# Top-32 attention into an MLP on one core: wider weight pieces, diagonals on another engine, other places for scores and values, and turns by DMA

## The chip, the core and the metric

The kernel runs on one core of one Trainium2 chip. The time is the device time of one execution in microseconds (us); the times before are given as the median of three runs. A core has these engines: PE (TensorE, matrix products; its weight loads are shown as PEld), DVE (VectorE), ACT (ScalarE), POOL (GpSimd) and SP (SyncE, which here only issues DMAs). Each works through its own queue of instructions in order, and waits where an instruction needs something that another engine or a DMA has not delivered yet.

## The reference

Inputs are q, k and v of 8 batches, 8 heads, 576 positions, 64 wide, and two weight matrices, `w_in` (512 x 2048) and `w_out` (2048 x 512). The weights come as 64-bit floats, all else as 32-bit floats.

```python
scores = scale * np.matmul(q, k.transpose(0, 1, 3, 2))
kth = np.partition(scores, -32, axis=-1)[..., -32:-31]
scores = np.where(scores >= kth, scores, -1e9)
attn = softmax(scores)                        # over the keys
x = np.matmul(attn, v)                        # (B,H,S,D) -> (B*S, H*D) = 4608 x 512
h = x @ w_in
g = np.where(h >= 1, h, np.where(h <= -1, 0.0, (h + 1) ** 2 / 4))
out = g @ w_out
```

Each query keeps its 32 largest scores of 576; the result of attention goes through a two-layer MLP.

## The kernel before

**Steps.** Attention is cut into 144 steps. A step is 128 queries of a pair of heads: its scores against 576 keys are two tiles of 128 x 576. Four steps (four head pairs) complete one chunk of 128 tokens by 512; there are 36 chunks. Batches go in pairs: four rounds of four steps for the first, two rounds of two steps for the last 64 queries of both (the tail rounds), four rounds of four steps for the second. A round's queries are turned (brought to columns) once.

**What a step does.** PE multiplies queries and keys into `sp` (L351), ACT scales that into `s` (L352). DVE takes the larger and the smaller of each column pair (`more` and `less`, L365, each reading two halves of `s`), and finds the largest scores eight at a time (MAX8 and MATCH_REPLACE8, L413 to L432), the 32nd by a scan (L444). ACT takes the exponential `e` (L388) with the negated maximum (`nmax`, L386). DVE masks `e` and sums it (L451), and inverts the sum (L397). What follows depends on the step. In the first nine ("early") steps and the last ones, ACT writes a diagonal matrix of the inverse sums (`diag`, L401), and PE multiplies the weights by it, which turns and divides them in one (`pw` L466, `pwt` L472); ACT copies the result to `wT` (L469, L473). In all others POOL divides (L404), ACT splits the words into 16-bit halves (`halves`, L481), and SP writes them to DRAM (`rows`, L483) and reads them back turned (`wT`, L484). Then PE multiplies values and weights (`po`, L498 and L506), and ACT copies that to a chunk's `xT` (L511).

**The MLP.** A chunk is 128 units of PE work. `hidden(x)` makes two products' worth of hidden values in a bank `ph` (L531), from which ACT makes `r` and `g` (L535, L542) and POOL the activation (L547 to L549); `final(f)` adds one product to `py` (L554), four hidden groups behind. `ph` and `po` share three banks. Units wait in a deque, `pending`.

**Weights.** They are converted from 64-bit words in pieces of 128 x 256 (64 pieces): ACT makes `units` (L145, L146), DVE `bits` (L154), POOL adds the two (L156). There are three buffers for each. `convert` issues the next piece's ACT part and the present piece's DVE and POOL part. Four pieces are done ahead of the first step; then each early step converts seven. While that lasts, the loads use eight rooms in the buffers `kT` and `v_in` (hence those names at L154 in the profile). Later each piece is loaded again and inspected (L171).

**The order of the work.** The order on PE, DVE, ACT and POOL is written out by hand: the program's order is each engine's order. A planner loop goes through the steps, each in seven slots. Per slot it issues one part of the step's selection on DVE, a conversion (early), and at fixed slots the transpose (slot 1), the values (slot 2) and the scores of step m + 2 (slot 4 in an early step, slot 2 otherwise); the queries and the next batch's keys are prepared at slot 6 or slot 1. At the end of each slot `advance` issues pending MLP units, as far as a share has come due and modelled times allow. In an early step the share is 48 units. SP's order (all DMAs) is not by hand: a scheduler sets it.

**Keys and queries.** For the first two batches PE turns the keys (`pk` L250, `pkt` L258, copied by ACT at L254 and L263) and the queries (`pq` L325, copied at L327). For later batches ACT splits them into halves (`parts`, L276, one buffer), SP writes `lines` (L278) and reads them turned (L279). The values' loads are issued among the turns of the keys.

Of the kernel before, what the change touches and what calls it, by code (L numbers as in the profile page):

```python
# [26 lines left out]
def kernel(  # L27
# [78 lines left out]
    WC = 256  # L106
    n_pieces = NK * DFF // WC + NF * DM // WC
    n_steps = B * (NT * NHP + NHP // 2)
    excess = const.tile([P, 2 * n_steps + n_pieces], F32, name="excess")
    signs = const.tile([P, 2, n_pieces], F32, name="signs")  # L110
# [15 lines left out]
    def load(pool, i, bufs=3):  # L126
        if i < n_pieces and i not in loaded:
            if room:
                loaded[i] = room[i % 8]
            else:  # L130
                loaded[i] = pool.tile([P, 2 * WC], U32, name="raw", bufs=bufs)
            nc.sync.dma_start(out=loaded[i], in_=pieces_of_weights[i][1].bitcast(U32))

    def words_of(pool, i, bufs=3):
        load(pool, i, bufs)
        words = loaded.pop(i).rearrange("p (n t) -> p n t", t=2)
        return words[:, :, 0], words[:, :, 1]

    def convert_piece(pool, i, any_size):

        lo, hi = words_of(pool, i)
        dst = pieces_of_weights[i][0]
        units = pool.tile([P, WC], F32, name="units", bufs=3)
        if not any_size:
            nc.scalar.activation(units, lo, AF.Identity, bias=one, scale=2.0 ** -52)  # L145
            nc.scalar.activation(units.bitcast(BF16).rearrange("p (n t) -> p n t", t=2)[:, :, 1], hi.bitcast(F32), AF.Sign)  # L146
        else:
            nc.scalar.activation(units, lo, AF.Identity, bias=two, scale=2.0 ** -51)
            sign = pool.tile([P, WC], F32, name="sign", bufs=3)
            nc.scalar.activation(sign, hi.bitcast(F32), AF.Sign)  # L150
        yield

        bits = pool.tile([P, WC], U32, name="bits", bufs=3)
        nc.vector.tensor_scalar(bits, hi, 3, None, ALU.logical_shift_left)  # L154
        if not any_size:
            nc.gpsimd.tensor_tensor(out=dst.bitcast(I32), in0=bits.bitcast(I32), in1=units.bitcast(I32), op=ALU.add)  # L156
        else:
            nc.gpsimd.tensor_tensor(out=bits.bitcast(I32), in0=bits.bitcast(I32), in1=units.bitcast(I32), op=ALU.add)
            size = pool.tile([P, WC], F32, name="units", bufs=3)
            nc.scalar.activation(size, hi.bitcast(F32), AF.Abs)  # L160
            nc.vector.scalar_tensor_tensor(out=sign, in0=size, scalar=TINY, in1=sign, op0=ALU.is_ge, op1=ALU.mult)

            nc.vector.tensor_scalar(bits.bitcast(F32), bits.bitcast(F32), LARGEST, -LARGEST, ALU.min, ALU.max)
            nc.gpsimd.tensor_tensor(out=dst, in0=sign, in1=bits.bitcast(F32), op=ALU.mult)
        yield

    def inspect_piece(pool, i):

        lo, hi = words_of(pool, i, 1)
        for x in range(2):  # L170
            nc.scalar.activation(lo.bitcast(F32), hi.bitcast(F32), AF.Sign, bias=tiny[:, x:x + 1],  # L171
                                 accum_out=signs[:, x, i:i + 1])


    def run(ctx, paired):
# [12 lines left out]
        def load_values(b):  # L188
# [6 lines left out]
            for j in range(2):  # L195
                nc.sync.dma_start(out=v_tl[0][j * TL:(j + 1) * TL, j::2, :],
                                  in_=v[b, j::2, SM:S, :].rearrange("h p d -> p h d"))
            for hp in range(NHP):
                g = hp % 2
                nc.sync.dma_start(out=v_tl[1][g * TL:(g + 1) * TL, 2 * hp:2 * hp + 2, :],  # L200
                                  in_=v[b, 2 * hp:2 * hp + 2, SM:S, :].rearrange("h p d -> p h d"))
            yield
# [69 lines left out]
        def turn(x, dst):  # L272
# [6 lines left out]
            nc.sync.dma_start_transpose(dst.bitcast(U16), lines.rearrange("p t k -> (p t) k"))  # L279

        def turned_keys_of(b):
# [15 lines left out]
            blocks = {0: load_block(0)}  # L297
            yield got
            for c in range(NT + 1):
                if c < NT:  # L300
                    blocks[c + 1] = load_block(c + 1)
                n = P if c < NT else TL
                turn(blocks.pop(c)[0:n], kT[:, :, c * P:c * P + n])
                if c == 1:
                    loads = load_values(b)
                    got["v"], got["v_tl"] = next(loads)
                if 1 <= c < NT:
                    next(loads)
                elif c == NT:
                    for _ in loads:  # L310
                        pass
                yield got
# [82 lines left out]
        def divide(st):  # L395
            rz = att.tile([P, 2], F32, name="rz")
            nc.vector.reciprocal(rz, st["z"])  # L397
            if st["by_tensor"]:
                st["rz"] = diag = (late or words).tile([P, 2, P], F32, name="diag", tag="halves", bufs=1)
                for i in range(2):  # L400
                    nc.scalar.activation(diag[:, i, :], ident, AF.Copy, scale=rz[:, i:i + 1])  # L401
# [75 lines left out]
        def move_w(st):  # L477
# [5 lines left out]
            nc.sync.dma_start(out=rows, in_=halves)  # L483
            nc.sync.dma_start_transpose(wT.bitcast(U16), rows.rearrange("p t k -> (p t) k"))  # L484
# [117 lines left out]
        def convert(time):  # L602
# [9 lines left out]
            for i in range(begun, converted + (7 if room else 3)):  # L612
                load(words, i)

        def inspect():
            nonlocal inspected
            if paired and inspected < n_pieces:
# [4 lines left out]
        K_TIME, PIECE_TIME, UNIT_TIME, SLOTS, EARLY_SHARE = 10.1, 0.55, 0.218, 7, 48  # L622
        pe_time, dve_time, done, scored, ready_at, usable = 9.0, 12.0, {}, {}, {}, {0: 0.0}

        def advance(amount, until):

            nonlocal spent, due, pe_time
            due = due + amount if pending else 0.0
            pe_time = max(pe_time, until - 4.0)
            while pending:  # L630
                cost, pieces, work, _ = pending[0]
                if pieces > converted or usable[pieces] > pe_time + 0.5:
                    break
                if due < cost or pe_time >= until:
                    break
                pending.popleft()
                due -= cost
                spent += cost
                pe_time += cost * UNIT_TIME
                work()  # L640
# [13 lines left out]
        if paired:  # L654
            for x in (stage.tile([P, NHP, S], F32, name="kT").rearrange("p h n -> p (h n)"),
                      stage.tile([P, H, NT, D], F32, name="v_in").rearrange("p h c d -> p (h c d)")):
                room.extend(x[:, c:c + 2 * WC].bitcast(U32) for c in range(0, 8 * WC, 2 * WC))
# [8 lines left out]
        prep = None  # L666
        state = []

        def queries(m):
            nonlocal pe_time  # L670
            if m < n and steps[m][0:2] not in qTs:
                r = steps[m][0:2]
                if r[0] > 1:
# [24 lines left out]
        for i in range(2, 8 if room else 3):  # L698
# [5 lines left out]
        for i in range(3):  # L704
            convert(13.0)
# [21 lines left out]
        for m in range(n + 2):  # L727
# [14 lines left out]
            if m < n:  # L742
# [3 lines left out]
                now_converting = range(SLOTS)  # L746
# [3 lines left out]
            for slot in range(SLOTS):  # L750
# [6 lines left out]
                elif slot == 3 and late is not None:  # L757
                    if m % 2:
                        inspect()
                    elif paired:  # L760
                        load(late, inspected, 1)
# [4 lines left out]
                if slot == 3 and 1 <= m <= n and state[m - 1] is not None and not state[m - 1]["by_tensor"]:  # L766
                    move_w(state[m - 1])
                    ready_at[m - 1] = done[m - 1] + 15.0
                if slot == 2 and m == n and paired:
# [5 lines left out]
                if slot == 2 and not early:  # L775
                    values_until((m - 2) // 2 * 2)
                if slot == (4 if early else 2):
                    begin_at(m + 2)
                if slot == (6 if early else 1):
                    queries(m + 3)  # L780
                    if (m < n and prep is None and next_keys < B and steps[m][0] == next_keys - 1 and steps[m][1] >= 1
                            and (next_keys > 1 or converted == n_pieces)):
                        prep = (turned_keys_of if next_keys > 1 else keys_of)(next_keys)
                    if prep is not None and (m % 2 == 0 or next_keys == 1):
                        got = next(prep, None)
                        pe_time += 0.5 if next_keys < 2 else 0.0
                        if got is None:
                            prep, next_keys = None, next_keys + 1
                        else:
                            keys[next_keys] = got  # L790
                advance((EARLY_SHARE if early else share) / SLOTS if m < n else 32.0, now)
# [52 lines left out]
```

## Time and profile before

| what | value |
|---|---|
| median of three runs | 1515.24 us |
| lowest and highest | 1515.05 and 1516.16 us |
| the profiled execution, its own time | 1516.81 us |
| the profile's span of it | 1514.6 us |
| mean granted clock of TensorE | 0.98 |
| moved by DMA | 259.76 MB, 172 GB/s |
| scans of DVE (L444), first, second and last | 24.83, 36.47 and 1440.08 us |
| end of PE's work | 1507.9 us |

The profile is of one execution. Its page gives the busy time of each engine, the span in 40 slices, the chain of work that ended last, and the costliest groups of instructions; further views answer by stretch of time, by wait (who waited, for whom, in total, how often, the longest), and by engine in order of time. A wait's releaser is inferred: it is the one that came last.

### The profile page before, as it was taken

What the parts mean: (1) busy time and instruction counts of PE and PEld (TensorE: products, weight loads), DVE (VectorE), ACT (ScalarE), POOL (GpSimd) and SP (SyncE); (2) the same over time, 40 slices, a digit from 0 to 9 for tenths busy, and PEclk for the clock granted to TensorE, in tenths of its full rate; (3) what the DMA queues carried; (4) which work ended last, traced back from release to release, by engine and by line L of the source; (5) the groups of instructions that cost most, each with busy time, mean ns of one, the idle gap of its engine ahead of it and who ended that gap; (6) DMA issues with size and microseconds to landing.
All of it is one profiled execution on the core that took longest, in us unless ns stands there. A gap on an engine that the chain in (4) does not pass through costs nothing.

```text
span 1514.6 us, 32180 instructions
## 1 busy us (share of the span) xinstructions
PE 1441.9 (95%) x10625; PEld 1042.8 (69%) x10625; DVE 1412.7 (93%) x4424; ACT 1167.1 (77%) x2288; POOL 921.8 (61%) x1339
## 2 busy tenths in 40 slices
PE   5588999999999999999999999899999999999998
PEld 4466677777777777677777777666677777777675
DVE  7888999999999999999999999999999999999912
ACT  7896878787778888787778888677777887777732
POOL 4563666666666666566666666566666666666630
PEclk7798999999999999999999999999999999999999
DMA  9542567775687777886677877786677777656510
GB/s 258 159 136 61 147 173 177 194 199 160 166 190 202 197 195 187 206 205 171 167 199 199 201 185 189 183 215 172 162 198 179 208 181 179 160 157 153 143 29 17
DMA packets 512448, 259.76 MB, mean 172 GB/s; under 512 B 459152, under 2 KB 467344, under 8 KB 512272
## 3 DMA queue, kind: packets, MB, share of 16 engines
q1 hardware_dynamic: 512272, 257.62, 65.6%
q8 instruction: 86, 1.41, 0.4%
q14 instruction: 90, 0.74, 0.2%
HBM read 62.91 MB, written 102.04 MB: 109 GB/s over the span
## 4 chain that ended last, share of the span: by engine, by line
PE 85%; ACT 8%; DMA 2%; issue 2%; POOL 1%; DVE 0%; SPq 0%; ACTq 0%; POOLq 0%; DVEq 0%
PE py L554 32%; PE ph L531 30%; PE sp L351 10%; PE po L498 10%; PE pw L466 2%; ACT halves L481 1%; ACT e L388 1%; ACT units L145 1%; PE po L506 1%; DMA rows<-halves 1%; ACT s L352 1%; DMA wT<-rows 1%; ACT wT L469 1%; ACT raw L171 0%; ACT g L542 0%
## 5 line engine op out<-in xcount | busy, mean ns | idle before, releaser
L531 PEld LDWEIGHTS ph<-xT,w_in 128*128 128x128 f32 x4608 | 547.0, 192 | 101.7 <-issue 82.2
L531 PE MATMUL ph<-xT,w_in 128*128 128x128 f32 x4608 | 557.2, 276 | 3.2 <-POOL w_in L156 3.1
L554 PE MATMUL py<-w_out,g 128*128 128x512 f32 x1152 | 551.0, 603 | 0.0
L547 POOL TENSOR_SCALAR r<-r 128x256 f32<-128x256 f32 x276 | 161.5, 585 | 447.2 <-ACT r L535 447.1
L372 DVE MATCH_REPLACE8 more<-tops,more 128x288 f32<-128x288 f32 x864 | 375.1, 437 | 0.0
L554 PEld LDWEIGHTS py<-w_out,g 128*128 128x128 f32 x1152 | 198.1, 191 | 181.2 <-issue 165.3
L481 ACT COPY halves<-e 128x1152 uint16<-128x1152 uint16 x266 | 291.9, 1143 | 15.5 <-DMA rows<-halves 14.5
L451 DVE SCALAR_TENSOR_TENSOR e<-s,kth,e 128x577 f32<-128x577 f32 x288 | 251.8, 909 | 3.6 <-ACT e L388 3.5
L549 POOL TENSOR_TENSOR g<-r,g 128x256 f32<-128x256 f32 x280 | 227.8, 814 | 22.0
L535 ACT ACTIVATE r<-ph,half 128x256 f32<-128x256 f32 (+1 forms) x296 | 136.1, 460 | 130.3 <-PE ph L531 104.2
L388 ACT ACTIVATE e<-s,nmax 128x576 f32<-128x576 f32 x288 | 222.4, 773 | 4.7
L404 POOL TENSOR_SCALAR e<-e,rz 128x576 f32<-128x576 f32 x266 | 223.4, 850 | 0.0
L352 ACT ACTIVATE s<-sp 128x576 f32<-128x576 f32 x288 | 172.0, 650 | 52.4 <-PE sp L351 51.9
L548 POOL TENSOR_TENSOR r<-r 128x256 f32<-128x256 f32 x276 | 191.3, 693 | 23.0
L351 PE MATMUL sp<-kT,qT 64*128 64x288 f32 x1024 | 162.9, 434 | 10.9 <-ACT kT L254 9.5
L498 PE MATMUL po<-wT,v_in 128*64 128x128 f32 x2048 | 143.4, 281 | 17.3 <-ACT g L542 15.3
L498 PEld LDWEIGHTS po<-wT,v_in 128*64 128x64 f32 x2048 | 117.0, 140 | 52.4 <-ACT g L542 40.1
L351 PEld LDWEIGHTS sp<-kT,qT 64*128 64x128 f32 x1024 | 89.4, 188 | 66.6 <-ACT r L535 25.0
L542 ACT ACTIVATE g<-ph,minus 128x256 f32<-128x256 f32 x280 | 130.1, 465 | 0.0
L413 DVE MAX8 tops<-more 128x8 f32<-128x288 f32 x288 | 125.4, 443 | 0.0
L365 DVE TENSOR_TENSOR less<-s 128x576 f32<-128x576 f32 x144 | 123.8, 860 | 0.0
L365 DVE TENSOR_TENSOR more<-s 128x576 f32<-128x576 f32 x144 | 109.9, 763 | 11.9 <-ACT s L352 11.9
(88 smaller groups left out, 1397.7 us busy)
## 6 DMA issues: line engine op xcount, KB each, us to landing
rows<-halves SPq DMA_DIRECT2D x133, 576.0 KB, 3.0
lines<-parts SPq DMA_DIRECT2D x48, 256.0 KB, 2.8
q_in<-in_q_dram SPq DMA_DIRECT2D x32, 256.0 KB, 4.0
kT<-in_moe_w_in_dram SPq DMA_DIRECT2D x32, 256.0 KB, 3.2
v_in<-in_moe_w_out_dram SPq DMA_DIRECT2D x32, 256.0 KB, 3.2
v_in<-in_v_dram SPq DMA_DIRECT2D x32, 256.0 KB, 4.2
raw<-in_moe_w_in_dram SPq DMA_DIRECT2D x32, 256.0 KB, 3.1
out_dram<-y SPq DMA_DIRECT2D x32, 256.0 KB, 3.2
```

The source lines that it names most:

```text
L351: nc.tensor.matmul(*x, start=True, stop=True)
L365: nc.vector.tensor_tensor(out=x, in0=s[:, :, 0:SH], in1=s[:, :, SH:S], op=op)
L372: nc.vector.match_replace(out=st["rest"][:, i, :], in_to_replace=eight(st["tops"], i, r - 8), in_values=src[:, i, :], imm_value=LOWEST)
L388: nc.scalar.activation(e[:, i, :], s[:, i, :], AF.Exp, bias=nmax[:, i:i + 1])
L404: nc.gpsimd.tensor_scalar(st["e"][:, i, :], st["e"][:, i, :], rz[:, i:i + 1], 1.0, ALU.mult, ALU.mult)
L451: nc.vector.scalar_tensor_tensor(out=st["all"][1][:, i, :], in0=st["all"][0][:, i, :], scalar=last[i], in1=st["all"][1][:, i, :], op0=ALU. ...
L481: nc.scalar.copy(halves[:, :, i * S:(i + 1) * S], st["e"][:, i, :].bitcast(U16).rearrange("p (k t) -> p t k", t=2))
L498: nc.tensor.matmul(po[j * D:(j + 1) * D], v_in[:, h, c, :] if c < NT else v_tl[0][:, h, :], wT[:, block(j, c)], start=(c == 0), stop=(c == ...
L531: nc.tensor.matmul(ph[:, i], w_in[:, kk, f * P:(f + 1) * P], xT[:, kk], start=(kk == 0), stop=(kk == NK - 1))
L548: nc.gpsimd.tensor_tensor(out=r, in0=r, in1=r, op=ALU.mult)
L549: nc.gpsimd.tensor_tensor(out=g, in0=r, in1=g, op=ALU.add)
L554: nc.tensor.matmul(py[0], gs[f // group][:, f % group], w_out[:, f, :], start=(f == 0), stop=(f == NF - 1))
```

## The change

1. Pieces of the weights are 512 wide: 32 pieces, two ahead of the first step, four in an early step (slots 0, 2, 4, 6), so eight early steps; four rooms for loads. The inspection keeps 256 (`parts=2`), and the modelled time of a piece becomes 0.9.
2. `diag` is written by GpSimd in place of ACT.
3. The scores of step m + 2 go out at slot 2 in every step, right behind the values.
4. Ahead of the values of a later step, at even m, pending units are issued until one final has gone out, if the last one was a hidden.
5. The turned read of `lines` is put off: it goes out at slot 3, or between a step's `rows` and its `wT`. The values' loads leave the keys' turns and go out in the steps that have none.
6. The second batch's keys are turned by DMA like those of later batches, and their preparation begins with the last early step; the queries are turned by DMA from the second late step on.

One more thing follows from 5: the six loads of the second batch's last 64 values are not issued in the changed program, because the third batch's loads take their place in `value_loads` first.

```diff
-    WC = 256
+    WC = 512
...
-    excess = const.tile([P, 2 * n_steps + n_pieces], F32, name="excess")
-    signs = const.tile([P, 2, n_pieces], F32, name="signs")
+    excess = const.tile([P, 2 * n_steps + 2 * n_pieces], F32, name="excess")
+    signs = const.tile([P, 2, 2 * n_pieces], F32, name="signs")
...
-    def load(pool, i, bufs=3):
-        if i < n_pieces and i not in loaded:
+    def load(pool, i, bufs=3, parts=1):
+        if i < n_pieces * parts and i not in loaded:
             if room:
-                loaded[i] = room[i % 8]
+                loaded[i] = room[i % len(room)]
             else:
-                loaded[i] = pool.tile([P, 2 * WC], U32, name="raw", bufs=bufs)
-            nc.sync.dma_start(out=loaded[i], in_=pieces_of_weights[i][1].bitcast(U32))
+                loaded[i] = pool.tile([P, 2 * WC // parts], U32, name="raw", bufs=min(bufs, 2))
+            c = i % parts * (WC // parts)
+            nc.sync.dma_start(out=loaded[i], in_=pieces_of_weights[i // parts][1][:, c:c + WC // parts].bitcast(U32))
...
-            nc.sync.dma_start_transpose(dst.bitcast(U16), lines.rearrange("p t k -> (p t) k"))
+            turns.append(partial(nc.sync.dma_start_transpose, dst.bitcast(U16), lines.rearrange("p t k -> (p t) k")))
+
+        turns = []
+
+        def finish_turns():
+            while turns:
+                turns.pop(0)()
...
             blocks = {0: load_block(0)}
+            got["loads"] = load_values(b)
+            got["v"], got["v_tl"] = next(got["loads"])
             yield got
...
-                if c == 1:
-                    loads = load_values(b)
-                    got["v"], got["v_tl"] = next(loads)
-                if 1 <= c < NT:
-                    next(loads)
-                elif c == NT:
-                    for _ in loads:
-                        pass
                 yield got
...
-                    nc.scalar.activation(diag[:, i, :], ident, AF.Copy, scale=rz[:, i:i + 1])
+                    nc.gpsimd.tensor_scalar(diag[:, i, :], ident, rz[:, i:i + 1], 1.0, ALU.mult, ALU.mult)
...
             nc.sync.dma_start(out=rows, in_=halves)
+            finish_turns()
             nc.sync.dma_start_transpose(wT.bitcast(U16), rows.rearrange("p t k -> (p t) k"))
...
-        K_TIME, PIECE_TIME, UNIT_TIME, SLOTS, EARLY_SHARE = 10.1, 0.55, 0.218, 7, 48
+        K_TIME, PIECE_TIME, UNIT_TIME, SLOTS, EARLY_SHARE = 10.1, 0.9, 0.218, 7, 48
...
+        def take():
+
+            nonlocal spent, due, pe_time, taken
+            cost, pieces, work, _ = pending[0]
+            if pieces > converted or usable[pieces] > pe_time + 0.5:
+                return False
+            pending.popleft()
+            due -= cost
+            spent += cost
+            pe_time += cost * UNIT_TIME
+            work()
+            taken = work.func
+            return True
...
-                if r[0] > 1:
+                if late is not None:
                     qTs[r] = turned_queries_of(q_ins[r], r[1])
...
-        for i in range(3):
-            convert(13.0)
+        convert(13.0)
...
-                now_converting = range(SLOTS)
+                now_converting = range(0, SLOTS, 2)
...
+                if slot == 3:
+                    finish_turns()
...
                 if slot == 2 and not early:
+                    if m % 2 == 0:
+                        while pending and taken is not None and taken.__name__ == "hidden" and take():
+                            pass
                     values_until((m - 2) // 2 * 2)
-                if slot == (4 if early else 2):
+                if slot == 2:
                     begin_at(m + 2)
                 if slot == (6 if early else 1):
                     queries(m + 3)
...
-                        prep = (turned_keys_of if next_keys > 1 else keys_of)(next_keys)
+                        prep = turned_keys_of(next_keys)
                     if prep is not None and (m % 2 == 0 or next_keys == 1):
                         got = next(prep, None)
-                        pe_time += 0.5 if next_keys < 2 else 0.0
                         if got is None:
                             prep, next_keys = None, next_keys + 1
                         else:
                             keys[next_keys] = got
+                            value_loads = got.get("loads", value_loads)
+                    elif value_loads is not None:
+                        next(value_loads, None)
```

## The prediction

> **What bounds the kernel now.** I read the page's shares first, then the table of stretches, the waits, and the timelines of single engines.
>
> ```profile
> PE 1441.9 (95%) x10625; PEld 1042.8 (69%) x10625; DVE 1412.7 (93%) x4424; ACT 1167.1 (77%) x2288; POOL 921.8 (61%) x1339
> ...
> PE 85%; ACT 8%; DMA 2%; issue 2%; POOL 1%; DVE 0%; SPq 0%; ACTq 0%; POOLq 0%; DVEq 0%
> ```
>
> PE and DVE are both nearly full, and the chain that ends last is PE's. The table of stretches (columns: stretch, then busy time of PE, PEld, DVE, ACT, POOL, then granted clock) shows two regimes:
>
> ```profile
> 20.00:40.00 20.00, 11.33 (x62) 7.45 (x60) 19.29 (x62) 17.77 (x39) 9.02 (x11) 0.59 0.84 249
> 40.00:60.00 20.00, 10.29 (x62) 8.51 (x63) 17.48 (x58) 17.62 (x42) 11.66 (x14) 0.75 0.57 174
> ...
> 120.00:140.00 20.00, 14.75 (x92) 11.30 (x89) 15.90 (x52) 14.51 (x35) 8.51 (x12) 0.83 0.13 36
> ...
> 400.00:600.00 200.00, 200.00 (x1534) 145.78 (x1534) 200.00 (x631) 164.06 (x314) 131.96 (x192) 1.00 0.75 192
> ```
>
> Up to about 181 us PE idles 2 to 10 us in every 20. Later, PE and DVE never stop. There, four steps take 38.16 us (py x8 begins at 417.45 and again at 455.61 on the chain), nearly all of it matmuls: 128 ph 14.3, 32 py 13.8, po 4.7, sp 4.7. So a gain can only be made before 181 us, in PE's work removed after it, or in the late waits:
>
> ```profile
> PE po L498 <- ACT g L542: 15.3, 8, 5.9
> PE po L506 <- DMA wT<-rows: 0.6, 1, 0.6
> PE sp L351 <- ACT qTt L327: 0.5, 1, 0.5
> ```
>
> These are all the waits of PE of weight from 181 to 1440 us (total, times, longest). The waits from 20 to 181 us name what binds there:
>
> ```profile
> PEld pw L466 <- ACT diag L401: 25.6, 6, 5.7
> PE pw L466 <- ACT diag L401: 22.3, 5, 5.3
> ...
> POOL w_in L156 <- ACT units L146: 15.1, 12, 3.6
> ...
> DVE bits L154 <- POOL w_out L156: 9.6, 9, 2.0
> ...
> DVE more L365 <- ACT s L352: 5.0, 2, 2.6
> ```
>
> ACT comes late with diag because conversions and two `e` are ahead of it; PE then stands before pw.
>
> **The loop of an early step.** The scan of DVE (L444) comes at 36.47, 49.05, 62.20, 74.88, so a step takes about 12.7 us. From one wT copy to the next the loop is ACT to diag (8.4 us: wT 1.2, nmax, two `e` 1.36, three to five pairs of units at 0.92, `s` 1.05, diag 0.6), then pw 3.8 at the low clock, then wT again.
>
> **Wide pieces.** No row is 512 wide, so I bound. ACT: 256 elements take 0.465 (L535), 576 take 0.773 (L388), 0.96 ns an element; the two units go from 0.512 and 0.493 to 0.756 and 0.739, and the pair's spacing from 0.92 to 1.41. A step has 4 x 1.41 = 5.6 in place of 7 x 0.92 = 6.4. DVE bits: 0.20 to 0.34, 1.4 a step either way. POOL: the add takes 0.73 alone at 256 and 0.20 for two columns (L407), so 1.25, 5.0 a step either way; the lower bound is 0.73, the upper 2 x 2.02 = 4.0, from the disturbed row below. I take 1.25, since most adds (first, third and fourth here, start, us, engine) run alone:
>
> ```profile
> 54.66 0.87 POOL L156 TENSOR_TENSOR w_out<-bits,units 128x256 int32<-128x256 int32 x1 [0.16 <-ACT units L146]
> 56.63 2.02 POOL L156 TENSOR_TENSOR w_in<-bits,units 128x256 int32<-128x256 int32 x1 [1.10 <-ACT units L146]
> ...
> 64.74 0.73 POOL L156 TENSOR_TENSOR w_out<-bits,units 128x256 int32<-128x256 int32 x1 [3.75 <-DVE bits L154]
> 66.45 0.73 POOL L156 TENSOR_TENSOR w_out<-bits,units 128x256 int32<-128x256 int32 x1 [0.98 <-ACT units L146]
> ```
>
> **Diagonals.** ACT is spared 0.6 a step. POOL gains two of 128 elements: between 0.10 (the smallest POOL row, a memset) and 0.40 each (256 elements alone, L547); I take 0.26, from L547's slope below. They queue behind the second wide add, and behind them wait excess and two more adds. New loop: ACT wT 1.2, nmax 0.26, `e` 0.68, units 1.41, xT 0.15, `s` 1.05, `e` 0.68, units 1.41, makes 6.85; then POOL add 1.25 and the first diag 0.3, then pw 3.8 and hand-over 0.4: 12.6. So no gain in steps 1 to 4: the wait of pw only changes its name.
>
> The Trainium skill ("SBUF — State Buffer", section "Who interferes with whom") says that GpSimd shares a read port with VectorE as an exclusive lock, and that a VectorE instruction with two SBUF inputs shuts out a GpSimd instruction that reads. The add at 56.63 agrees: it starts with L365's two pair operations (from 56.64, 0.76 each) and takes 2.02 for 0.73. By the rule, the add ahead of the diagonals pays 1.3 wherever it meets them; on all eight early steps that would be 10 us and the predicted time 1511.
>
> **Eight early steps, early scores.** With 32 pieces at four a step the early phase ends after eight steps instead of nine. The instruction orders of both programs have the same MLP work ahead of the scores of step 15 (220 units; a chunk's 128 take the 14.3 + 13.8 us above, so 0.219 us each), and the same from there to the end; but at the scores of step 10 the new one has 128 units done, the old one 96. From pw to scores right behind the values takes 6.62 (57.74 to 64.36). The eighth pw stands at 125.85 now, and I leave it there, as the loop is no shorter; scores of step 10 then come at 132.5 in place of 136.1: 3.6 us. Behind that, DVE's two waits for `s` (at 138.15 and 149.87, 5.0 us) may go, and the excess of steps 10 to 14 over the shortest step of 9.14 (2.2 us), since 7.0 us of PE work (32 units) and one pw group (2.0) are no longer there: a gain of 3.6 to 10.8, and if POOL is late, below nothing. I take 6, because new ACT work comes in here.
>
> **Keys and queries by DMA.** Gone from PE are the second batch's pk and pkt (four groups of 0.60 and one of 0.46, before step 15, inside the gain above) and seven pq groups; six of these lie behind step 15, where PE is full. The timeline shows them at 0.60, the tails at 0.46, with ends that overlap the next group; I count 0.45 each: 2.7 us. ACT pays twelve parts copies of 1.04 (12.5) for seventeen copies of 0.36 to 0.58 (9.0); ACT is at 77% and hides 3.5 us. A turn costs 1.04 on ACT, 2.8 to write lines, and 3.3 or 3.6 to transpose: 7 to 10 us with SP's issue, against a lead of a step or more (9 us). parts has one buffer, so two turns in a row wait 2.8 more. Taken at nothing; if it is late, scores of steps 12 to 14 wait up to 5 us. SP's own queue: each turn's transpose now stands behind the next rows write, so a wait of rows (256 us in all before transposes, hidden) no longer sits behind it; price nothing. Batch 1's six loads of the last 64 values are no longer issued in the new program, so those keys weigh in with zeros: this leaves out 0.2 MB of traffic, no time.
>
> **Values behind finals.** In the old order 28 of 70 value groups follow hiddens directly, in the new none: each follows a final (0.86 us of PE work, already there). A wait for ACT's g can be covered by one final: 8 x 0.86 = 6.9 of the 15.3. Four of the eight are 0.9 long and go; the long ones (2.5, 2.6, 5.9) come at the changes of batch, where halves stand for rows (14.5 us on ACT), and the moved value loads may or may not help them. Between 0 and 15.3; I take 5.
>
> **Sum.** Span 1514.6 - 6 - 2.7 - 5 = 1500.9. The profiled execution took 1516.81, 1.57 over the median, so the forecast for the median is 1515.24 - 13.7 = 1501.5, say 1501.
>
> **Rivals.** A measurement tells 0.2% (3 us) from no change.
> 1. Forecast, 1494 to 1507: 0.40.
> 2. Larger gain, 1482 to 1494: the freed ACT time shortens the early loop to DVE's own work (9.14 and 1.4 of bits, 10.5; 2.1 gained on each of steps 1 to 5, 10) and all 15 us of waits go: 1515 - 10 - 2.7 - 15 = 1487. For it: ACT is the wait's name now. Against: the loop counted above. 0.20.
> 3. The gain is hidden: the turned keys are late by 5 us, which eats the 6, and the long waits stay: 1515 - 1 - 2.7 - 3.5 = 1508, up to no change if queries come late as well. 0.20, of which 0.07 within 3 us. That an edit doesn't do what it says is part of this: the wait of pw only passes from ACT to POOL.
> 4. Slower: POOL binds the early phase. If wide adds meet the pair operations at the ratio of 2.02 to 0.73, the add ahead of the diagonals takes 3.5 (plus 2.2) and the two diagonals 0.7 each (plus 0.9): 3.1 a step, 25 in eight steps, 1501 + 25 = 1526. For it: DVE already waits 13 us for POOL's adds through the three bits buffers, and one step of 18.1 us (scans at 74.88 and 93.02) comes when POOL gets MLP work as well. It decides from a loop longer by 13.7 / 8 = 1.7 us. 0.20.
>
> Faster: 0.40 + 0.20 + 0.13 = 0.73; same 0.07; slower 0.20. Below 1484 I leave 0.07, above 1520 0.12.
>
> **What would show it.** Right: pw's waits name POOL diag instead of ACT, scans of steps 1 to 4 still 12.6 apart, the wide add near 1.25 alone, scores of step 15 near 175 us, four steps of 38.2 afterwards, po's wait for g well under 10 us. Wrong: adds of 2.5 or more ahead of diag, a step of 15 us in the first eight, sp waiting for kT or qT around 150 us, or a four-step period away from 38.2, which I take as unchanged and which weighs most: 0.4 us in it are 13 us.

## The result: slower, and the profile after

The changed kernel takes 1523.02 us (median of five runs, 1520.93 to 1523.30) against 1515.24 before: a ratio of 1.0059, 95% interval 1.0043 to 1.0075. In a second set of runs the ratio was 1.0069 (1.0044 to 1.0094). Forecast was 1501. The profiled execution of the changed kernel took 1520.93, the quickest of its five, so its span (1519.1) shows 4.5 us of the loss and the medians 7.8; the profile of the second set has 1522.5, and shows the same with larger sizes. Two executions of the experiments (3162.99 and 2449.00 us) lie far above all others of their kernels; ratios and medians leave them out.

The page's shares, and its chain by engine:

```profile
PE 1440.9 (95%) x10557; PEld 1036.1 (68%) x10557; DVE 1414.2 (93%) x4392; ACT 1154.6 (76%) x2196; POOL 921.4 (61%) x1329
...
PE 83%; ACT 4%; DMA 4%; DVE 4%; issue 2%; POOL 1%; SPq 1%; POOLq 0%; ACTq 0%; DVEq 0%
```

PE is as busy as before (1441.9), and the chain has 4% each of DVE and DMA on it, which had 0% and 2% before. The table of stretches, columns as above:

```profile
80.00:100.00 20.00, 16.32 (x128) 14.32 (x125) 13.85 (x40) 14.06 (x31) 14.39 (x20) 0.91 0.32 106
...
140.00:160.00 20.00, 13.81 (x96) 11.72 (x92) 19.32 (x60) 14.64 (x27) 6.57 (x10) 0.91 0.66 184
160.00:180.00 20.00, 13.55 (x88) 8.57 (x88) 17.18 (x55) 15.20 (x28) 11.29 (x18) 0.83 0.78 196
...
400.00:600.00 200.00, 199.87 (x1539) 144.96 (x1537) 200.00 (x626) 163.06 (x310) 129.46 (x187) 1.00 0.76 189
```

The late regime is the same: PE and DVE full, four steps in 38.2. The loss lies ahead of it. From 140 to 180 us PE works 27.4 us of 40; before, it worked 37.4. PE's account over the whole run closes: up to 180 us PE did 125.2 us of work in place of 134.2 (9.0 lost), from 180 to 1420 it stood 4.8 us less, behind 1420 it stood 1.5 us more, and it had 1.1 us less to do: 4.6, the later end of PE (1512.49 for 1507.85).

DVE's scans (L447 here, L444 before) place it by step:

| scan of step | before | changed | later by |
|---|---|---|---|
| 5 | 93.02 | 89.67 | -3.4 |
| 7 | 117.39 | 123.36 | 6.0 |
| 10 | 153.80 | 155.27 | 1.5 |
| 11 | 163.43 | 168.20 | 4.8 |
| 15 | 201.77 | 204.76 | 3.0 |
| 96 | 980.28 | 987.37 | 7.1 |
| 124 | 1259.90 | 1261.37 | 1.5 |
| end of PE | 1507.85 | 1512.49 | 4.6 |

So there was a gain to step 5, a loss of 9 us in steps 6 and 7, a gain, a loss of 3 at step 11, a slow loss to step 96 (2.5 of its 4.1 between steps 60 and 68, at the change of batches), a gain of 5.6 from 1000 to 1260 us, and a longer end. The waits of 20 to 181 us that bear on this, in order, and PE's first from 181 to 1445 us:

```profile
POOL r L551 <- ACT r L539: 31.4, 5, 10.1
...
PE pw L469 <- POOL diag L404: 22.0, 6, 5.3
...
DVE more L368 <- ACT s L355: 7.7, 7, 2.8
...
PE pw L469 <- ACT units L147: 5.7, 1, 5.7
```

```profile
PE po L502 <- ACT g L546: 7.8, 3, 3.8
PE pw L469 <- POOL diag L404: 3.1, 1, 3.1
```

pw waits for POOL as long as it did for ACT (22.3), and 5.7 us more at its first, which the profile puts down to ACT's units. The wait of po for g has halved (15.3 before).

**The fifth pw shows how the diagonals come late.** DVE's row of the sum's inverse for step 4, POOL's timeline from there on, and PE's (start, us, engine, line, tile), with PE's of the kernel before last:

```profile
79.29 0.14 DVE L400 RECIPROCAL rz<-z 128x2 f32<-128x2 f32 x1
```

```profile
84.10 0.40 POOL L551 TENSOR_SCALAR r<-r 128x256 f32<-128x256 f32 x1 [6.40 <-ACT r L539]
...
85.97 1.27 POOL L157 TENSOR_TENSOR w_out<-bits,units 128x512 int32<-128x512 int32 x1
...
90.40 1.79 POOL L157 TENSOR_TENSOR w_out<-bits,units 128x512 int32<-128x512 int32 x1
92.15 0.91 POOL L549 TENSOR_SCALAR r<-r 128x256 f32<-128x256 f32 x1
93.14 0.77 POOL L553 TENSOR_TENSOR g<-r,g 128x256 f32<-128x256 f32 x1
93.90 0.72 POOL L404 TENSOR_SCALAR diag<-ident,rz 128x128 f32<-128x128 f32 x2
```

```profile
94.33 3.55 PE L469 MATMUL pw<-diag,e 128*128 128x128 f32 x16 [3.68 <-POOL diag L404]
```

```profile
87.19 2.01 PE L466 MATMUL pw<-diag,e 128*128 128x128 f32 x16
```

The diagonal's input is there at 79.29; the diagonal is written at 93.90, when POOL has been through four groups of MLP work and two wide adds. The first of the groups waits 6.40 us for ACT's `r`; behind it POOL has no idle time up to the diagonal. pw itself takes 3.55 in place of 2.01, at a lower granted clock (0.91 from 80 to 100 us and 0.58 from 94 to 98, 1.00 in both before). Before, the fifth pw began at 87.19 and the eighth at 125.85; now at 94.33 and 135.05. The delay does not begin there. The first pw is 3.3 us late already (35.17 for 31.92): its first diagonal, behind a wide add, took 1.46 us beside DVE's pair operations, where 0.37 is usual. The fourth pw is 3.9 late, the fifth 7.1, the eighth 9.2.

### The profile page after: what moved, and what is told of

It reads as the page before. It is cut to its first block, busy times and chain, and to the rows that moved or that the text cites. A ratio compares the mean times of both kernels' runs of the same rounds, so it can differ in the third digit from the quotient of the medians.

```text
span 1519.1 us, 31855 instructions
## 1 busy us (share of the span) xinstructions
PE 1440.9 (95%) x10557; PEld 1036.1 (68%) x10557; DVE 1414.2 (93%) x4392; ACT 1154.6 (76%) x2196; POOL 921.4 (61%) x1329
## 4 chain that ended last, share of the span: by engine, by line
PE 83%; ACT 4%; DMA 4%; DVE 4%; issue 2%; POOL 1%; SPq 1%; POOLq 0%; ACTq 0%; DVEq 0%
PE ph L535 30%; PE py L558 30%; PE sp L354 10%; PE po L502 9%; PE pw L469 2%; DMA rows<-halves 1%; PE po L510 1%; ACT halves L484 1%; DVE more L375 1%; DMA wT<-rows 1%; DMA lines<-parts 1%; DVE e L454 1%; ACT e L391 1%; ACT s L355 1%; ACT wT L472 0%
## 5 line engine op out<-in xcount | busy, mean ns | idle before, releaser
L551 POOL TENSOR_SCALAR r<-r 128x256 f32<-128x256 f32 x276 | 151.7, 550 | 454.5 <-ACT r L539 454.5
L484 ACT COPY halves<-e 128x1152 uint16<-128x1152 uint16 x268 | 293.8, 1143 | 13.0 <-DMA rows<-halves 12.4
L454 DVE SCALAR_TENSOR_TENSOR e<-s,kth,e 128x577 f32<-128x577 f32 x288 | 264.0, 952 | 1.7 <-ACT e L391 1.6
L553 POOL TENSOR_TENSOR g<-r,g 128x256 f32<-128x256 f32 x280 | 236.0, 843 | 22.0
```

The lines of the kernel that those rows point to most:

```text
L454: nc.vector.scalar_tensor_tensor(out=st["all"][1][:, i, :], in0=st["all"][0][:, i, :], scalar=last[i], in1=st["all"][1][:, i, :], op0=ALU. ...
L484: nc.scalar.copy(halves[:, :, i * S:(i + 1) * S], st["e"][:, i, :].bitcast(U16).rearrange("p (k t) -> p t k", t=2))
L553: nc.gpsimd.tensor_tensor(out=g, in0=r, in1=g, op=ALU.add)
```

## The experiments

The theory, from this profile: the diagonals cost by their place in POOL's queue, the rest of the early change gains. The first rival: POOL is simply full there, whoever writes the diagonals. Ratios are to the kernel before, run on the same chip, with 95% intervals; one thousandth is 1.5 us. Each ratio compares kernels on one chip; kernels that are set beside each other below often ran on different ones. Where keys stay by DMA, the last 64 values of the second batch are left out as in the change: zeros stand in their place, so its output lacks their part.

**The changed kernel again.**

> The changed kernel once more, beside the others of this call, as their base line. Ratio to before 1.004 to 1.007; scans and the end within 2 us of the profile on record.

Measured: 1.0069 (1.0044 to 1.0094). Fifth and eighth pw at 93.68 and 137.23, end of PE at 1515.94. The two profiles of this one kernel differ by 3.3 us at scan 15, 4.9 at scan 61 and 3.4 at the end of PE. A smaller difference between the profiles of two kernels shows nothing alone.

### Diagonals

**By ACT again.**

```diff
-                    nc.gpsimd.tensor_scalar(diag[:, i, :], ident, rz[:, i:i + 1], 1.0, ALU.mult, ALU.mult)
+                    nc.scalar.activation(diag[:, i, :], ident, AF.Copy, scale=rz[:, i:i + 1])
```

> The changed kernel with the diagonals written by ACT again, all else as changed. Queue theory: on POOL the diagonals stand behind adds and MLP work of the same step, which made steps 6 and 7 last 17.4 and 16.3 us and the two last pw 3.2 us later; with ACT these steps fall to about 13 and the end is 3 us shorter: together 8 to 11 us under the changed kernel, a ratio to before of 0.999 to 1.001. Rival (POOL is full in these steps with wide adds and MLP work, whoever writes the diagonals): steps 6 and 7 stay above 15, only the end gains 3 us, ratio 1.004.

Measured: 0.9968 (0.9953 to 0.9982), 9 to 10 thousandths (14 to 15 us) under the changed kernel, more than expected. ACT's timeline and PE's have the diagonal and the fifth pw at

```profile
86.79 0.69 ACT L404 ACTIVATE diag<-ident,rz 128x128 f32<-128x128 f32 x2
```

```profile
87.24 2.05 PE L469 MATMUL pw<-diag,e 128*128 128x128 f32 x16 [0.17 <-ACT diag L404]
```

and the eighth pw at 125.41. The scan of step 15 is 9.3 us earlier than in the changed kernel, 6.3 earlier than before. Step 7 fell from 16.3 to 12.4 us, as expected; step 6 stays at 17.1, which was not. The long step was step 5 before (18.1 us) and is step 6 here, whoever writes the diagonals. So of the 9.3 us that the changed kernel loses against the kernel before in steps 6 and 7, 5.1 are lost here too. What the diagonals cost arises by scan 5 (3.6), in steps 6 and 7 (4.2) and in step 8 and behind it (1.5). The end, from the last scan to the end of PE, takes 70.3 us in place of 71.0, not 68: that part of the expectation failed.

**By ACT, with the same two operations kept on POOL, into a tile nobody reads.**

```diff
+                    nc.scalar.activation(diag[:, i, :], ident, AF.Copy, scale=rz[:, i:i + 1])
+                    nc.gpsimd.tensor_scalar(spare[:, i, :], ident, rz[:, i:i + 1], 1.0, ALU.mult, ALU.mult)
```

> The changed kernel with the diagonals that PE uses written by ACT, and the same two operations on POOL kept at their place in its queue, written to a spare tile that nobody reads. Queue theory (what costs is that PE waits for an operation that stands behind POOL's adds and MLP work): pw at the times of the kernel with ACT's diagonals (fifth pw at 87, eighth at 125), ratio 0.997. Rival (POOL's load and its contention with VectorE cost): times of the changed kernel (fifth pw at 94, eighth at 135), ratio 1.005.

Measured: 0.9989 (0.9973 to 1.0006). The fifth and eighth pw are at 87.51 and 125.77, while POOL, in the same queue, reaches its copy only at

```profile
91.44 0.71 POOL L406 TENSOR_SCALAR spare<-ident,rz 128x128 f32<-128x128 f32 x2
```

POOL's load and its contention with DVE are still there, and the time is 8 thousandths (12 us) under the changed kernel of the same set (1.0069). So the operation on POOL costs little; PE's wait for its place in the queue is what costs. The rival falls. This kernel lies 2 thousandths over the one without the copies; the intervals overlap.

**By ACT in the last two steps alone.**

```diff
+                    if late is None:
                         nc.gpsimd.tensor_scalar(diag[:, i, :], ident, ...)
+                    else:
+                        nc.scalar.activation(diag[:, i, :], ident, AF.Copy, scale=rz[:, i:i + 1])
```

> The changed kernel with the diagonals of the last two steps alone by ACT, the early ones by POOL. Queue theory: 2 to 4 us under the changed kernel at the end, from the last scan to the end of PE 67 to 68 us in place of 71, ratio 1.003 to 1.004; scans before it unchanged. Rival (the end is longer because PE has more work left there): no change, ratio 1.006.

Measured: 1.0034 (1.0017 to 1.0051). By the ratio 2.5 to 3.5 thousandths less, but the intervals overlap, and the trace does not have it: from the last scan to the end 70.3 us in place of 71.0. pw waits 2.1 us in place of 3.1 there and then others wait (1.55 for wT by DMA). Inconclusive, at most 1 us by the trace; why the end is some 2 us longer than before (67.8) stays open.

### Finals ahead of values

**The changed kernel without the rule.** Its three lines at slot 2 (from `if m % 2 == 0`) are taken out.

> The changed kernel without the rule that a final goes out ahead of the values. If that rule is what took the wait of 0.9 us in every four steps between 1000 and 1160 us away, the four-step period there is 39.1 again and the time 4 to 6 us above the changed kernel, ratio 1.009 to 1.010. Rival (the period there changed because the phase of the work shifted, or the finals cost as much elsewhere, as the 0.5 us that every other step is longer suggests): no change, ratio 1.005 to 1.007.

Measured: 1.0020 (1.0006 to 1.0035), 4 to 5 thousandths under the changed kernel, where more time was expected. The period from 1040 to 1260 us is 38.2 to 38.3 without the rule too. And step 11, 12.9 us with the rule, takes 10.0. PE's timeline with the rule, and without:

```profile
142.13 5.62 PE L535 MATMUL ph<-xT,w_in 128*128 128x128 f32 x48
150.17 2.05 PE L535 MATMUL ph<-xT,w_in 128*128 128x128 f32 x16 [2.41 <-ACT g L546]
155.73 3.51 PE L535 MATMUL ph<-xT,w_in 128*128 128x128 f32 x16 [3.51 <-ACT g L546]
159.03 1.25 PE L558 MATMUL py<-w_out,g 128*128 128x512 f32 x2
160.21 1.24 PE L354 MATMUL sp<-kT,qT 64*128 64x288 f32 x8
```

```profile
143.48 5.62 PE L535 MATMUL ph<-xT,w_in 128*128 128x128 f32 x48
151.82 1.24 PE L354 MATMUL sp<-kT,qT 64*128 64x288 f32 x8 [2.72 <-DMA qT<-lines]
```

At step 10 a fresh chunk stands first in the deque, with no final near. "Until a final has gone out" sends two more groups of hidden products ahead of the scores, each waiting for a bank that ACT's g must free (2.41 and 3.51): the scores of step 12 begin at 160.2, without the rule at 151.8, where what ends the wait is qT. DVE, at step 11, then waits for `s` of step 12:

```profile
163.74 0.86 DVE L368 TENSOR_TENSOR more<-s 128x576 f32<-128x576 f32 x1 [2.83 <-ACT s L355]
```

In these two profiles that is made up one step later (scan 12 at 177.33 with the rule, 177.17 without). The 2.9 us by which PE ends earlier without it arise at the first change of batches, where scan 61 follows scan 60 by 9.5 us in place of 13.9. So the drain is seen, but that it is what the rule costs here is not shown.

**The kernel before with the rule alone** (`take` and the three lines).

> The kernel before with the rule alone that a final goes out ahead of the values. By the prediction a wait of 0.9 us each is covered, 5 us under before, ratio 0.997. By the run without the rule (the changed kernel lost nothing without it, it gained), the waits at 1026 to 1143 us go here too, but the stalls at the changes of batch near 633 and 986 us are 1 to 2 us longer each: ratio 0.999 to 1.001.

Measured: 0.9973 (0.9956 to 0.9990): here the rule gains 2.7 thousandths, 4 us. PE's waits for g from 190 to 1440 us fall from 15.3 in 8 times to

```profile
PE po L498 <- ACT g L542: 4.9, 3, 4.5
```

The four waits of 0.9 us are gone, and the two of 2.5 are down to 0.2; waits for wT by DMA and for `y` are 4.6 us longer. So the rule does what the prediction said, where those waits are; in the changed kernel the order of hiddens and finals has a pair of finals ahead of po without it (before: a run of 48 ph, then po at 478.1 us; changed, without the rule: such a run, two py, then po at 482.7). In the traces 27 of 77 runs of po directly follow hidden products before, 1 with the rule added, and none of 76 in the changed kernel, with the rule or without.

**The rule only from step 20 on, diagonals by ACT; and no rule, diagonals by ACT.**

> The changed kernel with diagonals by ACT and the rule of the finals only from step 20 on. Drain theory (at step 10 the rule sends some forty hidden products ahead of the scores of step 12, because a fresh chunk has no final ready): step 11 near 10 us, 3 us under the twin with the rule everywhere (0.997), so 0.994 to 0.995; the stall at the first change of batches stays 3 to 4 us longer than without the rule. Rival (the rule costs at the changes of batch alone): 0.997.

> The changed kernel with diagonals by ACT and without the rule of the finals; keys and queries by DMA as changed. If the cost of the changed kernel is the diagonals (9 thousandths) and the rule (4) and nothing else of weight, ratio 0.992 to 0.994, step 11 near 10 us in place of 12.9. Rival (the turned keys cost 3 us more, as they seemed to in the run with keys by PE alone): 0.996.

Measured: 0.9972 (0.9955 to 0.9988) and 0.9970 (0.9951 to 0.9989), both no better than with the rule everywhere (0.9968). Step 11 is 10.0 us in both, against 12.9: the drain is shown. But of the 2.1 and 2.5 us gained by scan 11, 0.6 and 1.0 are left at scan 12, and by scan 64 both kernels are 4 us behind. Four steps across the first change of batches (60 to 64) take 44 to 45 us in these two profiles and 42.3 in the one with the rule. That stall takes 42.7 and 44.6 in the two profiles of the changed kernel, and without the rule 39.4 with diagonals by POOL and 45.1 by ACT, which differ in nothing near it. What sets it stays open, and here it is as large as what the rule costs.

### Queries and keys by DMA

**The changed kernel with the first two batches' queries by PE as before.**

```diff
-                if late is not None:
+                if r[0] > 1:
                     qTs[r] = turned_queries_of(q_ins[r], r[1])
```

> The changed kernel with the first two batches' queries by PE as before, nothing else undone. If queries by DMA cost 6 us in the changed kernel too, 4 to 6 us under it: ratio 1.001 to 1.003. Rival (what PE is spared counts, the run before was one happy order): 1.007 to 1.009.

Measured: 1.0003 (0.9984 to 1.0022), 6 thousandths under the changed kernel. **With diagonals by ACT and no rule of the finals:**

> The changed kernel with diagonals by ACT, without the rule of the finals, and with the first two batches' queries turned by PE as before. If six groups of pq on a full PE cost 0.45 each, 2 to 3 us over its twin with queries by DMA. Rival (ACT and SP take back what PE is spared, as the wait of 2.7 us for qT ahead of the scores of step 12 suggests): within 1 us, or 1 to 3 us under it.

Measured: 0.9907 (0.9883 to 0.9930), 6 thousandths under its twin (0.9970). This is the quickest version here: 1502.59 us, the median of five runs; by the ratio it is 14 us under the kernel before. **With the rule kept:**

> Diagonals by ACT, queries of the first two batches by PE, the rule of the finals kept. Drain theory: the rule costs 2 to 3 us at step 10 and little else, so 2 to 3 us over the twin without it, 0.992 to 0.993, step 11 near 13 us. Rival (it pays at the changes of batch what it costs there): equal, 0.990 to 0.991.

Measured: 0.9941 (0.9923 to 0.9959), over the one without by 3 thousandths; the intervals overlap slightly. Step 11 takes 10.8 us, not the 13 expected: with queries by PE the drained groups wait 1.1 us for g in place of 5.7. So the drain costs most where ACT comes late with g. Against diagonals by ACT alone (0.9968), queries by PE gain 3 thousandths here, with intervals that overlap.

ACT's timeline of the changed kernel shows what a turned query does where keys are turned as well:

```profile
143.25 1.05 ACT L279 COPY parts<-q_in 128x1024 uint16<-128x1024 uint16 x1 [0.29 <-DMA lines<-parts]
147.25 1.04 ACT L279 COPY parts<-k_block 128x1024 uint16<-128x1024 uint16 x1 [2.95 <-DMA lines<-parts]
148.20 1.18 ACT L355 ACTIVATE s<-sp 128x576 f32<-128x576 f32 x2
```

`parts` has one buffer. Two turns in a row leave ACT standing 2.95 us, with `s` of step 11, the next g and halves behind it. DVE does not wait for that `s`; what comes late is g, for which the drained groups wait, and with them the scores of step 12 (160.2; with queries by PE 156.0). With queries by PE, ACT comes to `s` of step 11 1.0 us after parts of its one key turn, DVE waits 0.52 us for `s` of step 12 in place of 2.83, and scan 11 follows scan 10 by 10.8 in place of 12.9 or 13.5.

**The second batch's keys by PE.** Alone; with diagonals by ACT; and with diagonals by ACT, queries by PE and no rule:

```diff
-                        prep = turned_keys_of(next_keys)
+                        prep = (turned_keys_of if next_keys > 1 else keys_of)(next_keys)
```

> The changed kernel with the second batch's keys turned by PE as before (its six loads of the last 64 values are issued again with them); queries still by DMA. Turn theory: ACT no longer stands for the one parts buffer at 143 to 150 us, step 11 falls from 12.9 to about 10 and scores of step 12 come 3 to 5 us earlier, wT of step 9 too: 3 to 5 us under the changed kernel, ratio 1.003 to 1.004. Rival (the stretch is set by PE's and DVE's work, and pk and pkt add 2.9 us to it): no gain or 3 us more, ratio 1.006 to 1.008.

> The changed kernel with the diagonals by ACT and the second batch's keys by PE (its six loads of values issued again). If the two add as they did alone (0.997 and 3 thousandths under the changed kernel), ratio 0.993 to 0.995, and scores of step 15 at 170 to 173 us. Rival (with ACT writing the diagonals the handover is set by something else, such as the first wT by DMA): as with the diagonals alone, 0.996 to 0.998.

> Diagonals by ACT, no rule of the finals, keys and queries of the first two batches by PE: what is left of the change is wide pieces, early scores and the queue order. If the keys by DMA cost nothing of weight (as with ACT's diagonals before), within 2 us of the kernel with queries alone by PE, 0.990 to 0.992. Rival (keys by PE cost pk and pkt, 2.9 us, on a PE that is full by then): 0.992 to 0.994.

Measured: 1.0029 (1.0016 to 1.0042), 0.9964 (0.9951 to 0.9977), and 0.9964 (0.9947 to 0.9981). In the first it gains 3 to 4 thousandths over the changed kernel; in the second nothing; in the third it loses 6 thousandths against keys by DMA (0.9907). In this last kernel scores wait 3.58 us for ACT's kT at 149.59. So keys by DMA pay if nothing else turns beside them. The first run's gain was not in step 11 (13.9 us there), where I expected it; with the drain known, that is no surprise.

**No rule, diagonals by ACT, keys by PE, queries by DMA.**

> The kernel with diagonals by ACT and keys by PE, without the rule of the finals. Shift theory (the early phase alone leaves another order of hiddens and finals in which a pair of finals stands ahead of po anyway, so the rule has nothing to cover in the changed kernel and costs 3 us at the first change of batches): 3 to 5 us under its twin with the rule, no waits of 0.9 us from 1020 to 1150 us. Rival (what the rule is worth hangs on chance of order): the waits of 0.9 us come back, 4 to 6 us over its twin.

Measured: 0.9938 (0.9917 to 0.9959), 2.6 thousandths under its twin with the rule (0.9964), with no waits of 0.9 us in the late stretch. The intervals overlap slightly. With this kernel all four ways of turning are there, for diagonals by ACT and no rule:

| | queries by DMA | queries by PE |
|---|---|---|
| second batch's keys by DMA | 0.9970 | 0.9907 |
| second batch's keys by PE | 0.9938 | 0.9964 |

Queries by PE gain 6 thousandths beside keys by DMA and lose 2.6 beside keys by PE, the latter with overlapping intervals. So it is the two turns together that cost; queries by DMA alone are not shown to.

### Pieces, scores, queue order

**Pieces of 256 again** (seven a step, nine early steps), with diagonals by ACT and keys by PE: `WC = 256`, four pieces ahead, eight rooms, slots 0 to 6, 0.55.

> The kernel with diagonals by ACT and keys by PE, with pieces of 256 again: seven in an early step, nine early steps. If wide pieces carry the early gain (the loop saves 0.8 us of ACT a step, one step by PE fewer, 28 more units done by step 9), scans from step 15 on are 4 to 6 us later than its twin's, ratio 0.997 to 0.999. Rival (the early scores carry it): within 2 us of its twin.

Measured: 0.9989 (0.9973 to 1.0006) against 0.9964 for its twin: wide pieces may be worth some 2.5 thousandths; the intervals overlap. In the traces scan 15 is 3.2 us later with narrow pieces and the end of PE 2.8, which is no more than two profiles of one kernel differ by.

**Early scores at slot 4 again**, diagonals by ACT and keys by PE.

> The kernel with diagonals by ACT and keys by PE, with early scores at slot 4 as before. If early scores carry part of the gain: DVE waits for s again (2.5 us each) in the early steps, scans from step 10 on 3 to 5 us later than its twin's, ratio 0.996 to 0.998. Rival (the wide pieces carry it): within 2 us of its twin.

Measured: 0.9977 (0.9963 to 0.9992) against 0.9964: within the noise; scan 15 is 1.6 us later, the end 1.9, and scan 10 only 0.4 where 3 to 5 were expected.

**The kernel before with the queue order alone.**

> The kernel before with the queue order alone: turned reads of keys and queries put off, and values loaded in steps without a key turn. The stretch from 1000 to 1160 us, where before lost 0.9 us in every four steps, is quicker in the changed kernel even without the rule of the finals. If the queue order does that, the waits of po for g at 1026 to 1143 us go, four steps take 38.3 there, and the time is 4 to 6 us under before, ratio 0.996 to 0.997. Rival (the phase that the earlier stretch leaves behind decides it): they may stay, ratio 0.999 to 1.001.

Measured: 1.0004 (0.9988 to 1.0020): nothing, and the waits of 0.9 us at 1025 to 1142 us stay.

## Why the prediction was wrong, point by point

- **Diagonals: the step that failed.** The prediction walked the loop of steps 1 to 4, where POOL has only adds, found 12.6 us, and left the eighth pw at 125.85 "as the loop is no shorter". The loop held (pw of steps 1 to 3 are 12.7 us apart), but it began 3.3 us late, at the first pw. From step 4 on POOL carries MLP work as well, and a diagonal stands behind all of it; the prediction had seen this work arrive ("when POOL gets MLP work as well") and left it out of the sum. Measured: eighth pw 9 us later (135.05; with diagonals by ACT 125.41), and 14 us in all between the two ways of writing it. A diagonal takes 0.37 on POOL, not 0.26, which hardly matters. The rival "POOL binds the early phase" had the engine and the size (1526), but priced adds that meet the pair operations (3.5 each); the wide adds ran at 1.27 when alone and 1.79 at most in the rows above (2.29 once in the whole phase), so it was mostly the queue, not the contention, which shows at the first pw (1.1 us). The rule of the Trainium skill ("SBUF — State Buffer", "Who interferes with whom") that the prediction weighed fits single rows, such as that 1.79, which starts while DVE's masking operation with two inputs runs (90.20), but not the loss.
- **Wide pieces and early scores: right, in size too.** 6 us were forecast at step 15. With these two and the queue order alone (diagonals by ACT, keys and queries by PE, no rule) scan 15 is 6.0 earlier than before and the ratio 0.9964; with all of the change except that ACT writes the diagonals it is 6.3 earlier. How the gain divides between the two is not shown: 3 and 2 us by the traces, no more than two profiles of one kernel differ by. The sizes were right as well: an add took 1.27 (1.25 forecast), the two units 0.76 and 0.78 (0.756 and 0.739). "No row is 512 wide" is not so: ACT's copies of pw to wT are.
- **Queries by DMA: wrong in sign beside keys by DMA.** 2.7 us of PE work gained was counted, the late turn "taken at nothing", though the text had the price: "two turns in a row wait 2.8 more". Undoing it gains 6 thousandths (9 us) in two pairs and 3 in a third, and loses 2.6 in a fourth, where keys are by PE too. In the traces of the first pair, 2.4 us stand at scan 11 and 2.4 at scan 15 by the changed kernel's first profile, 4.4 and 5.7 by its second; of the second pair, 2.5 at scan 15, and about half of the rest arises between scans 60 and 64, for which no cause is shown.
- **Values behind finals: right for the kernel before, wrong for the changed one.** 5 us were forecast, 4 measured, in a kernel that has the waits. The changed kernel's other order has lost them already, so the gain cannot be had twice, and the rule drains a chunk's hidden products ahead of the scores at step 10, which the prediction did not ask: it priced one final at 0.86 and not what must go out ahead of it. That the rule costs 4 to 5 thousandths in the changed kernel is measured; how much of it is the drain is not shown, as step 12 makes most of it up, and with ACT's diagonals and both turns by DMA undoing the rule gained nothing (0.9968 and 0.9970).
- **Keys by DMA: PE's work inside the gain of 6, the turns taken at nothing;** measured between a cost of 4 and a gain of 6 thousandths, by what else is turned beside them.
- **Queue order: price nothing, measured nothing.**
- **The four-step period**, which weighed most, stayed at 38.2 as assumed.
- **The signs.** Of those for being right, pw waits for POOL's diagonals, the add near 1.25, the period and po's wait for g (7.8) came; the scans of steps 1 to 4 came 12.4, 11.5, 11.4 and 12.7 apart in place of 12.6, and the scores of step 15 at 186.2 in place of 175 (176.2 with diagonals by ACT). Of those for being wrong, steps of 15 us and more came (15.2, 17.4 and 16.3 for steps 5 to 7).

The sum then reads, from the forecast of -13.7: diagonals +14, queries about +9 instead of -2.7, the rule about +6 instead of -5. These do not add up exactly (they would give +23, and +8 was measured), as the effects overlap: the rule and the queries share the stretch from 130 to 180 us, where undoing either shortens step 11 (to 10.0 and 10.8), and the stall at the first change of batches moves with all of them. How much each overlap takes is not shown. That the quickest version reaches the forecast ratio (0.9907; 1501 of 1515.24 is 0.991) is chance: it has neither the queries by DMA nor the rule that the forecast counted 7.7 us for.

## What to carry to other kernels

Moving an operation to another engine moves it into that engine's queue: list everything issued ahead of it there in the busiest step of the phase, not in the first ones, with what each of those waits for in turn. A rule of the form "issue until X has gone out" has the price of all that may have to go out ahead of X. And a gain counted as removed waits should be checked against the other parts of the same change, which may have moved those waits already.

## What was not expected of the hardware

- The operation that writes a diagonal takes about the same on POOL and ACT: 0.72 for the pair on POOL (93.90), 0.69 on ACT (86.79). Where it ran beside the masking operation on DVE (L454), one of them took 1.12 on POOL at 109.24, and DVE's own, 0.81 elsewhere, 0.91 (108.95); the one before, beside a wide add, took 1.45 (107.57).
- PE's clock: sixteen pw after a wait of 3.68 us took 3.55 us at a granted clock of 0.58, sixteen after 0.17 us took 2.05. The wait was paid twice there. It is not so each time: after 2.51 us (109.31 in the changed kernel) they took 2.27, and after 2.48 in its second profile (109.60) 3.59.
